# A 1 KB load ahead of the first weight load of a one-token decode kernel

## The chip, the core and the metric

The kernel runs on one core of a Trainium2 chip. The core has a matrix engine (TensorE, PE in the profile), a vector engine (VectorE, DVE), a scalar engine (ScalarE, ACT), GpSimd (POOL) and SyncE (SP), and 16 DMA engines that bring data from HBM into on-chip memory. The metric is device time in microseconds (us); less is better. "ns" is written where nanoseconds are meant.

## What is computed

One token goes through two branches that are mixed by a gate. Branch A is attention over the last 4096 positions of a key and value cache (32 query heads, 8 cache heads of 128); branch B is a gated two-layer network. Everything is in bf16.

```
def _A_ref(x, k_cache, v_cache, wq, wo):            # x 1x512
    W = min(4096, max(256, Sk // 4))                # 4096 of 65536
    q = (x @ wq).reshape(B, Sq, 32, 128) ...
    k, v = last W positions of the caches, each head repeated 4 times
    scores = einsum("bhqd,bhkd->bhqk", q, k) * (Dh ** -0.5)
    return (softmax(scores) @ v) ... @ wo           # 4096x512
def _B_ref(x, w_gate, w_up, w_down):                # 512x1792, 512x1792, 1792x512
    return (sigmoid(x @ w_gate) * (x @ w_up)) @ w_down
g = sigmoid((x * gate_w).sum(-1, keepdims=True))
return g * a + (1 - g) * b
```

With a single token there is hardly any reuse: each of the 30.67 MB of weights and cache is read from HBM once and used once.

## The kernel before

All large loads are issued by SP on one queue (`dq = nc.sync`, L78), in the order in which they are needed; each DMA engine works through its share of them in that order. The order is:

- `wq_sb` (L81): the query weights, 4 MB. `wq_v` lays them out so that partition p holds rows 4p to 4p+3 of the matrix, 32 KB in one piece.
- four `kn` (L85, called from L92): the keys, 2 MB each, two cache heads to a load.
- `wg_sb` (L95), `wu_sb` (L99) and four small `wx_sb` (L106): the two input weights of branch B.
- three `vv` (L85, from L116), then half of `wo_sb` (L118), the last `vv` in two halves (L119, L120) and the other half of `wo_sb` (L121). `vv` uses the four buffers of `kn` again (pool `blk`), so a `vv` load waits until the transposes of that `kn` are done.
- four pieces of `wd_sb` (L126), the last of them one eighth of the first.

ACT issues two loads of 1 KB on a queue of its own: x (L75) and `gate_w` (L76), both into `xr`. At the end SP and ACT each store half of the result (L367, L369).

The compute follows the loads. PE turns x into columns (L156, L163), DVE works out the gate (L173 on), and when `wq_sb` has landed PE makes q (L208). Then come the transposes of the keys on DVE (L196), the scores on PE (L235), branch B's products (L251), the softmax, the products with the values (L319), and at the end the rows of `wo_sb` and `wd_sb` (L306) summed into one result row, which DVE and ACT copy out (L366, L368).

Small tiles that live all through the kernel come from the pool `const`, one buffer each; `xr` is one of them. Tile names, pools and waits on semaphores are handled by the tile framework; only the order on PE, DVE and ACT is written out by hand (from L185 on).

Of the kernel before, what the change touches and what calls it, by code (L numbers as in the profile page):

```python
# [12 lines left out]
BF16 = mybir.dt.bfloat16  # L13
# [4 lines left out]
def kernel(  # L18
# [16 lines left out]
    P = 128  # L35
# [27 lines left out]
    const = ctx.enter_context(tc.tile_pool(name="const", bufs=1))  # L63
# [14 lines left out]
    dq = nc.sync  # L78
    wq_sb = big.tile([P, DC, HQ * DH], BF16, name="wq_sb", tag="big")
    wq_v = A_wq.rearrange("(p c) n -> p c n", c=DC)  # L80
    dq.dma_start(wq_sb[:], wq_v)  # L81


# [316 lines left out]
```

## Time and profile before

| what | value |
|---|---|
| median of 5 runs | 80.77 us (80.68 to 82.05) |
| the profiled execution's own time | 80.74 us |
| its span, first to last instruction | 79.1 us |
| granted TensorE clock, mean | 0.957 |
| busy: PE, DVE, ACT, POOL | 70%, 50%, 14%, 5% |
| bytes on SP's load queue | 30.67 MB in 2754 packets |
| HBM read over the span | 388 GB/s |

The span is smaller than the time, because the time also has what lies ahead of the first and behind the last instruction. The profile cuts the span into 40 equal slices and gives the busy share of each engine in tenths; the row DMA is the mean over the 16 DMA engines. An instruction that issues a DMA is listed under its engine with a q (SPq, ACTq): its time is the issuing alone, not the transfer. In a table of stretches the columns are: length, busy time of PE, PEld (weight loads of PE), DVE, ACT and POOL with their number of instructions, granted clock, DMA share, and GB/s; the bytes of a packet are counted in the stretch in which it starts.

### The profile page before, as it was taken

What the parts mean: (1) busy time and instruction counts of PE and PEld (TensorE: products, weight loads), DVE (VectorE), ACT (ScalarE), POOL (GpSimd) and SP (SyncE); (2) the same over time, 40 slices, a digit from 0 to 9 for tenths busy, and PEclk for the clock granted to TensorE, in tenths of its full rate; (3) what the DMA queues carried; (4) which work ended last, traced back from release to release, by engine and by line L of the source; (5) the groups of instructions that cost most, each with busy time, mean ns of one, the idle gap of its engine ahead of it and who ended that gap; (6) DMA issues with size and microseconds to landing.
All of it is one profiled execution on the core that took longest, in us unless ns stands there. A gap on an engine that the chain in (4) does not pass through costs nothing.

```text
span 79.1 us, 825 instructions
## 1 busy us (share of the span) xinstructions
PE 55.8 (70%) x324; PEld 25.6 (32%) x324; DVE 39.2 (50%) x51; ACT 11.4 (14%) x21; POOL 3.7 (5%) x13
## 2 busy tenths in 40 slices
PE   0200092999980799988899662999799569998940
PEld 0200041334420234433333230444244513475710
DVE  0600920009738999999995727999900200001020
ACT  2400000142675000000000248000200000020010
POOL 7910000000000000000000000000000000000000
PEclk9999999999999559999999999999999955999999
DMA  7599799999999999999999999999999999999700
GB/s 183 199 414 498 315 497 398 398 423 447 456 398 423 447 456 398 444 406 418 438 415 414 431 456 406 423 431 456 414 414 406 414 452 435 414 394 399 294 7 1
DMA packets 2762, 30.71 MB, mean 388 GB/s; under 512 B 324, under 2 KB 584, under 8 KB 840
## 3 DMA queue, kind: packets, MB, share of 16 engines
q1 hardware_dynamic: 2754, 30.67, 92.6%
q8 instruction: 2, 0.03, 0.2%
q10 hardware_dynamic: 6, 0.00, 0.0%
HBM read 30.67 MB, written 0.00 MB: 388 GB/s over the span
## 4 chain that ended last, share of the span: by engine, by line
DMA 91%; SPq 3%; PE 1%; DVE 1%; issue 0%
DMA kn<-in_A_k_cache_dram 38%; DMA wd_sb<-in_B_w_down_dram 30%; DMA vv<-in_A_v_cache_dram 24%; SPq L85 2%; PE a_ps L306 1%; SPq L81 1%; DVE res L366 1%
## 5 line engine op out<-in xcount | busy, mean ns | idle before, releaser
L235 PE MATMUL S_ps<-kT,qbig 128*128 128x512 bf16 x64 | 16.3, 407 | 3.9 <-DVE qbig L224 2.8
L319 PE MATMUL pv_ps<-vv,eT 128*32 128x512 bf16 x64 | 15.9, 405 | 3.3 <-DVE eT L280 1.4
L196 DVE STREAM_TRANSPOSE kT<-kn 128x2048 f32<-128x2048 f32 x8 | 17.8, 2279 | 0.0
L235 PEld LDWEIGHTS <-qbig 128*128 128x128 bf16 x64 | 6.5, 102 | 13.7 <-issue 4.5
L208 PE MATMUL q_ps<-wq_sb,xT 128*128 128x512 bf16 x32 | 9.8, 483 | 1.5 <-DMA wq_sb<-in_A_wq_dram 1.5
L319 PEld LDWEIGHTS <-eT 128*32 128x32 bf16 x64 | 6.3, 101 | 11.9 <-issue 3.8
L213 DVE STREAM_TRANSPOSE qtT<-q_sb 128x512 f32<-128x512 f32 x4 | 2.8, 700 | 8.2 <-ACT q_sb L210 8.2
L331 DVE TENSOR_TENSOR oT<-o_ps,rb 128x16 bf16<-128x16 f32 x2 | 0.3, 175 | 12.6 <-PE o_ps L330 12.6
L208 PEld LDWEIGHTS <-xT 128*128 128x128 bf16 x32 | 3.8, 120 | 7.9 <-issue 5.9
L190 PE MATMUL S_ps<-ident,other 2*128 2x512 bf16 x4 | 2.0, 610 | 6.0 <-DVE other L148 6.0
L210 ACT CAST q_sb<-q_ps 128x512 bf16<-128x512 f32 x8 | 4.7, 586 | 8.3 <-PE q_ps L208 8.3
L306 PE MATMUL a_ps<-wo_sb,oY 128*1 128x256 bf16 x64 | 4.8, 272 | 0.3 <-DVE oY L339 0.3
L325 ACT COPY pv_sb<-pv_ps 64x512 f32<-64x512 f32 x2 | 1.2, 579 | 19.4 <-PE pv_ps L319 19.4
L280 DVE STREAM_TRANSPOSE eT<-e_sb 128x1024 bf16<-128x1024 bf16 x2 | 2.4, 1224 | 1.9 <-ACT e_sb L278 1.9
L262 ACT ACTIVATE sge<-gu_ps 128x448 f32<-128x448 f32 x1 | 0.5, 544 | 18.9 <-PE gu_ps L251 18.9
L306 PEld LDWEIGHTS <-oY 128*1 128x1 bf16 x64 | 2.8, 83 | 1.2 <-DVE oY L339 0.4
L173 DVE TENSOR_TENSOR gpr<-xr 1x512 f32<-1x512 bf16 x1 | 0.7, 680 | 4.8 <-DMA xr<-in_gate_w_dram 4.8
L290 DVE RECIPROCAL sg<-sge 128x448 f32<-128x448 f32 x1 | 3.0, 2952 | 0.0
L257 DVE TENSOR_REDUCE pm<-S_ps 128x1 f32<-128x1024 f32 x2 | 2.4, 1204 | 0.9 <-PE S_ps L235 0.9
L156 PE MATMUL xt_ps<-ident,xr 1*128 1x1 bf16 x4 | 0.3, 166 | 3.5 <-POOL ident L132 3.5
L190 PEld LDWEIGHTS <-other 2*128 2x128 bf16 x4 | 0.6, 158 | 6.3 <-DVE other L148 6.1
L366 DVE CAST res<-a_ps 1x256 bf16<-1x256 f32 x1 | 0.4, 411 | 4.0 <-PE a_ps L306 4.0
(63 smaller groups left out, 34.7 us busy)
## 6 DMA issues: line engine op xcount, KB each, us to landing
kn<-in_A_k_cache_dram SPq DMA_DIRECT2D x4, 2048.0 KB, 27.8
vv<-in_A_v_cache_dram SPq DMA_DIRECT2D x3, 2048.0 KB, 18.6
wq_sb<-in_A_wq_dram SPq DMA_DIRECT2D x1, 4096.0 KB
wo_sb<-in_A_wo_dram SPq DMA_DIRECT2D x2, 2048.0 KB
vv<-in_A_v_cache_dram SPq DMA_DIRECT2D x2, 1024.0 KB
wg_sb<-in_B_w_gate_dram SPq DMA_DIRECT2D x1, 1792.0 KB, 33.5
wu_sb<-in_B_w_up_dram SPq DMA_DIRECT2D x1, 1568.0 KB
wd_sb<-in_B_w_down_dram SPq DMA_DIRECT2D x1, 1024.0 KB
```

The lines of the kernel that those rows point to most:

```text
L85: dq.dma_start(t[:, n0:n1, :].rearrange("p n d -> p (n d)"), cache[0, 2 * a:2 * a + 2, SBASE:SBASE + W, :] .rearrange("y (x n) d -> x y n ...
L190: nc.tensor.matmul(S_ps[u // 2][:, u % 2, :], lhsT=other[:].rearrange("p o y u -> p (o y u)"), rhs=ident[0:2, 0:2].rearrange("p (o y) -> p ...
L196: nc.vector.transpose(t[:].bitcast(F32), kn[a][:, v * KB:(v + 1) * KB, :] .rearrange("p n d -> p (n d)").bitcast(F32))
L208: nc.tensor.matmul(q_ps[:], lhsT=xT[:, c:c + 1].to_broadcast([P, P]), rhs=wq_sb[:, c, ks], start=(c == 0), stop=(c == DC - 1))
L210: nc.scalar.copy(q_sb[:, ks], q_ps[:])
L213: nc.vector.transpose(qtT[:].bitcast(F32)[:, kq], q_sb[:].bitcast(F32)[:, kq])
L235: nc.tensor.matmul(S_ps[v][:, hb, :], lhsT=q_st[:, a, dhi, :, t], rhs=k_v[:, hb * 16:(hb + 1) * 16, dhi, :, t], start=False, stop=(a == HP ...
L257: nc.vector.tensor_reduce(pm2[:, v:v + 1], S_ps[v][:].rearrange("p a b -> p (a b)"), axis=AX.X, op=ALU.max)
L280: nc.vector.transpose(eT[:, :, v * KB:(v + 1) * KB, :].rearrange("p a n r -> p n a r"), e_sb[:, v, :].rearrange("p (n a r) -> p n a r", a= ...
L290: nc.vector.reciprocal(sg[:], sge[:])
L306: nc.tensor.matmul(a_ps[32 * i:32 * i + 1, i, 0:HN], lhsT=lhsT, rhs=rhs[:, i * HN:(i + 1) * HN], start=start, stop=stop)
L319: nc.tensor.matmul(pv_ps[32 * (a % 2):32 * (a % 2) + 32, a // 2, :], lhsT=eT[:, a, 4 * m:4 * m + 4, :].rearrange("p n r -> p (n r)"), rhs= ...
```

## The change

A tile of 32 bf16 columns, `first`, is taken from the pool `const`. Ahead of the load of `wq_sb`, SP issues a load of 64 bytes into each of 16 of its partitions (every eighth), from the beginning of the rows of `wq_v` that belong to those partitions. Nothing reads the tile. All else stays as it is.

```
     wq_sb = big.tile([P, DC, HQ * DH], BF16, name="wq_sb", tag="big")
     wq_v = A_wq.rearrange("(p c) n -> p c n", c=DC)
+    first = const.tile([P, 32], BF16, name="first")
+    dq.dma_start(first[0:P:8, :], wq_v[0:P:8, 0, 0:32])
     dq.dma_start(wq_sb[:], wq_v)
```

More of the change, by code (lines that the diff above doesn't have):

```diff
@@ L80 @@
     wq_v = A_wq.rearrange("(p c) n -> p c n", c=DC)
+    first = const.tile([P, 32], BF16, name="first")
+    dq.dma_start(first[0:P:8, :], wq_v[0:P:8, 0, 0:32])
     dq.dma_start(wq_sb[:], wq_v)
```

## The prediction

> **What bounds the kernel now.** I read the page's slices first, then the chain of waits, then that chain in order of time, and last the opening microseconds as a timeline and as stretches of 0.25 us.
>
> ```profile
> DMA  7599799999999999999999999999999999999700
> GB/s 183 199 414 498 315 497 398 398 423 447 456 398 423 447 456 398 444 406 418 438 415 414 431 456 406 423 431 456 414 414 406 414 452 435 414 394 399 294 7 1
> ```
>
> Each digit is 1.98 us. From the third slice to the 37th the 16 DMA engines are busy without a hole. Only the first two slices move less than 200 GB/s; the rest stay around 420.
>
> ```profile
> DMA 91%; SPq 3%; PE 1%; DVE 1%; issue 0%
> DMA kn<-in_A_k_cache_dram 38%; DMA wd_sb<-in_B_w_down_dram 30%; DMA vv<-in_A_v_cache_dram 24%; SPq L85 2%; PE a_ps L306 1%; SPq L81 1%; DVE res L366 1%
> ...
> 33.11 18.62 DMA vv<-in_A_v_cache_dram
> 51.75 23.83 DMA wd_sb<-in_B_w_down_dram
> 75.58 0.04 issue
> 75.62 0.66 PE a_ps L306 x6
> 76.28 0.40 DVE res L366
> ```
>
> The chain is one queue of loads: 30.67 MB through SP's queue, the last rows of wd landing at 75.58, and only 0.66 us of matmuls, a 0.40 us copy and the output store behind it. PE (70%) and DVE (50%) have slack everywhere. So whatever moves the whole stream of loads by some time moves the end by that time, and whatever stays beside the stream costs nothing. The change stands at the head of that stream.
>
> ```profile
> 0.73 0.51 ACTq L75 DMA_DIRECT2D xr<-in_A_x_dram  x1
> 0.74 0.41 SPq L81 DMA_DIRECT2D wq_sb<-in_A_wq_dram  x1
> 1.21 2.59 SPq L85 DMA_DIRECT2D kn<-in_A_k_cache_dram  x4
> 1.28 0.21 ACTq L76 DMA_DIRECT2D xr<-in_gate_w_dram  x1
> ```
>
> ```profile
> 1.50:1.75 0.25, 0.00 (x0) 0.00 (x0) 0.00 (x0) 0.22 (x1) 0.25 (x1) 1.00 0.01 4
> 1.75:2.00 0.25, 0.00 (x0) 0.00 (x0) 0.01 (x1) 0.25 (x1) 0.25 (x1) 1.00 6.35 1573
> 2.00:2.25 0.25, 0.00 (x0) 0.11 (x1) 0.25 (x2) 0.25 (x1) 0.25 (x1) 1.00 1.01 262
> ...
> 3.75:4.00 0.25, 0.19 (x2) 0.10 (x2) 0.00 (x0) 0.00 (x0) 0.25 (x3) 1.00 2.77 1180
> 4.00:4.25 0.25, 0.00 (x0) 0.00 (x0) 0.00 (x0) 0.00 (x0) 0.25 (x2) 1.00 1.24 524
> ...
> 5.00:5.25 0.25, 0.00 (x0) 0.00 (x0) 0.00 (x0) 0.00 (x0) 0.00 (x0) 1.00 3.39 1442
> ```
>
> The last column counts a packet's bytes where it starts. 1573 GB/s for 0.25 us is 393 KB, twelve packets of 32 KB (one partition's row of wq each): twelve of the 16 engines begin their first packet at 1.75 to 2.00. Their second packets begin at 3.75 to 4.25 (1180 and 524 are nine and four packets), the third at 5.00 to 5.25. A first packet thus takes about 2.0 us and a second about 1.25: the stream loses some 0.75 us in its first packet. That is what the tiny load could touch. The line at 1.50 holds x's single kilobyte (4 GB/s): it runs at once and its readers start at 1.99.
>
> **The change, part by part.** It adds one SP instruction ahead of L81, 16 rows of 64 bytes, and a 64-byte column of the const pool. Nothing is removed, nothing reads the tile.
>
> *The issue on SP.* Everything on SP behind it moves: wq, four kn, wg, wu, the wx, vv, wo, wd and the output store. Only wq's move matters, because from kn on the issues lead the data by microseconds (wu is issued by 4.93, 14 MB stand ahead of it, some 30 us). The trace holds no issue of 16 rows. The nearest rows:
>
> ```profile
> L126 SPq DMA_DIRECT2D wd_sb<-in_B_w_down_dram x4: 328/328/430, 43.9 to 56.6; - x4
> L106 SPq DMA_DIRECT2D wx_sb<-in_B_w_up_dram x4: 676/694/822, 13.5 to 23.3; - x4
> L367 SPq DMA_DIRECT2D out_dram<-res x1: 278/278/278, 76.7 to 76.7; - x1
> ```
>
> The smallest issue on SP is 0.28 us (one row), two plain dimensions as here give 0.33 (wd), and wx, with its many-dimensioned source, 0.69. Between two issues lies 0.06 (1.15 to 1.21). The first issue of a queue seems dearer: on ACT the same form took 0.51 first and 0.21 second. If a part of wq's 0.41 is of that kind, it goes over to the tiny load and wq falls to the 0.34 of wo_sb's first half. So the delay is at least 0.28 + 0.06 - 0.07 = 0.27 and at most 0.82 + 0.06 = 0.88. I take the row that is nearest in form, wd: 0.33 + 0.06 - 0.04 (half of that saving) = 0.35 us. It lies bare on the path: no byte of the queue can flow before wq's issue.
>
> *The tiny packets.* One packet and one count of the semaphore per engine. x's load has the same 1 KB in all and ran in the line at 1.50, 0.3 to 0.5 us after its issue's end; the tiny rows will run at about 1.5 to 1.7, wq's first row at 1.8 + 0.35 = 2.15. They are over by then: 0. If they were not, a 1 KB packet is the nearest thing: the last wd rows have that size, and at the 294 GB/s of the slice near the end one on each engine, 16 KB, takes 0.06 us.
>
> *The semaphore turn.* SP already stops for earlier loads: L106's first issue waits 8.6 us, from 4.93 to 13.51, for wq. The loads seem to share a set of semaphores in turn, and one more load at the front shifts who waits for whom: wg, wu or wx may now wait for x, gate_w or the tiny load. Behind that wait stand wx, vv and the rest. x lands by 1.99 and gate_w by 8.06, when its reader starts, both before 13.51, and some 30 us of queued bytes cover the stop: 0. With that cover gone a stop for gate_w would cost up to 3 us.
>
> *Other engines.* wq lands 0.35 later (13.5 to 13.85), so the q matmuls start later, and so do the transposes that free the kn buffers for vv. vv's first issue at 28.47 still has over 10 us of queued bytes ahead: 0. gate_w may slip in ahead of wq's packets and free DVE sooner, off the path: 0.
>
> *The first packet.* What it becomes is the unknown. Bounds: it keeps its 2.0 us (0), or falls to the second's 1.25 (-0.75); slower than 2.0 is not excluded, but a packet that begins in as full a rush as now has no reason to be. I take 0, for two reasons. x's load, on a cold engine and a cold queue, showed no slow start: 0.75 us from its issue's end (1.24) to its readers (1.99). So what is slow is not the first touch but the first rush, 16 engines asking for 32 KB rows at the same moment, and the tiny load leaves that rush as it is, 0.35 us later. Second, if a first touch did cost 0.75 us, the tiny load would have to sit it out itself, on the same engine and ahead of wq, so little could be won.
>
> The Trainium skill, page "DMA: Bandwidth & Descriptors", section "Anatomy of one DMA", puts a fixed cost of about 2.0 us on each DMA of the GpSimd path, most of it the confirmation of the write, and its rules call transfers under 64 KB overhead. Were that cost in series with the queue, the sum would be 82.7; x's load took 1.26 us from issue to reader here, and 22 loads on one queue leave no hole in the slices, so it overlaps. The same page, "Latency and other measured facts", has an HBM access at 0.2 us on average and 2 us under high load; that reading of the slow first packet leaves it slow, and leaves the sum at 81.1.
>
> **Sum.** 80.74 (span 79.1 and 1.64 around it) + 0.35 + 0 + 0 + 0 = 81.09. The profiled run is 0.03 below the median of the runs, 80.77, so 81.1 stands for either.
>
> **The rivals.**
>
> *The first packet becomes a normal one* (faster). Place: the first descriptor of wq on each engine. Price: -0.75 + 0.35 = -0.40, 80.35. It decides once more than 0.35 of the 0.75 is saved. For it: every engine's second packet is quick, though the rush of 16 goes on. Against: x's quick load.
>
> *A start-up time that runs from the first touch* (same). The tiny load, issued in 0.33 where wq takes 0.41, touches HBM some 0.08 us earlier, the wait of 0.75 runs while SP issues wq, and wq's first packet ends 0.08 us sooner or as now: 80.66 to 80.8. For it: 0.35 is less than 0.75, so the whole delay could hide. Against: x again, and the twelve engines' near-equal first packets whichever of them had carried x.
>
> *A dear first issue* (slower yet). If 16 strided rows are described like wx, the delay is 0.69 + 0.06 = 0.75: 81.5. For it: ACT's first issue of 0.51. Against: two plain dimensions.
>
> *The load does nothing at all*, since its packets and issue hide in the start: excluded on SP, whose issues run back to back from 0.74.
>
> **How the numbers follow.** The main forecast has 0.52, the normal first packet 0.22, the start-up time from first touch 0.18, the dear issue 0.08. The likeliest gives 81.1, its own range 80.95 to 81.4. To leave no more than 2 in 10 out the range goes down to the full saving and up to the dear issue: 80.3 to 81.5. A measurement tells about 0.3%, 0.24 us, from no change. Slower by more: 0.52 and 0.08, less some 0.05 for a short issue: 0.55. Faster by more: 0.22 plus a little of the start-up case: 0.24. The rest, 0.21, is within.
>
> **What would show it.** SP's first line should be the tiny issue at 0.74, about 0.33 long, wq's at about 1.13. Stretches of 0.25 us should show twelve or more first packets at about 2.1 and the second ones 2.0 later, at 4.1 to 4.4; wq's readers should start near 13.9 and the last of wd land near 75.9. If second packets begin 1.25 after the first, the forecast is wrong by the saving; if wq's issue is not later than 1.0, by the delay. A stall of SP that empties the queue, seen as a hole in the DMA row after the second slice, would undo all of it.

## The result and the profile after

The changed kernel is slower. Over 44 runs its median is 82.57 us (81.37 to 82.87) against 80.86 us (80.49 to 82.06) over 79 runs of the kernel before; the ratio is 1.0112, with a 95% interval of 1.0094 to 1.0130, that is 0.9 us. Executions of every kernel here but e10 fall into two groups some 1 us apart (23 of these 44 and 20 of these 79 into the upper one), so the medians given below are those of the lower group: 81.64 against 80.81, 0.83 us more. The forecast was 81.1 us with a range of 80.3 to 81.5: the direction was right, the size was not, and the time lies outside the range by either median as by the ratio (80.8 x 1.0112 = 81.7).

The profile of the changed kernel (82.69 us, span 81.0) first as SP's issues, in the columns start, length, engine and line:

```profile
0.73 0.63 SPq L82 DMA_DIRECT2D first<-in_A_wq_dram  x1
1.42 0.57 SPq L83 DMA_DIRECT2D wq_sb<-in_A_wq_dram  x1
2.04 2.60 SPq L87 DMA_DIRECT2D kn<-in_A_k_cache_dram  x4
...
5.84 18.51 SPq L108 DMA_DIRECT2D wx_sb<-in_B_w_up_dram  x4
```

The tiny load takes 0.63 us to issue, and wq behind it 0.57 instead of 0.41. wq's issue ends at 1.99 instead of 1.15: 0.84 us later, made of 0.63, a gap of 0.06 and 0.16 for wq's own issue, less 0.01 of an earlier start. The same kernel in stretches of 0.25 us (last column: GB/s, a packet's bytes counted where it starts):

```profile
2.00:2.25 0.25, 0.00 (x0) 0.10 (x1) 0.25 (x2) 0.25 (x1) 0.25 (x1) 1.00 0.04 2
2.25:2.50 0.25, 0.00 (x0) 0.00 (x0) 0.25 (x2) 0.25 (x1) 0.25 (x1) 1.00 0.04 6
2.50:2.75 0.25, 0.00 (x0) 0.00 (x0) 0.25 (x2) 0.25 (x1) 0.25 (x1) 1.00 4.01 1049
2.75:3.00 0.25, 0.00 (x0) 0.00 (x0) 0.25 (x3) 0.03 (x1) 0.25 (x1) 1.00 2.52 655
...
4.50:4.75 0.25, 0.10 (x1) 0.10 (x2) 0.23 (x3) 0.00 (x0) 0.00 (x0) 1.00 2.16 918
4.75:5.00 0.25, 0.25 (x1) 0.25 (x1) 0.00 (x0) 0.00 (x0) 0.00 (x0) 1.00 2.48 1049
...
5.75:6.00 0.25, 0.25 (x2) 0.12 (x1) 0.21 (x2) 0.00 (x0) 0.00 (x0) 1.00 2.47 1049
6.00:6.25 0.25, 0.25 (x2) 0.00 (x0) 0.22 (x2) 0.00 (x0) 0.00 (x0) 1.00 2.15 918
```

The tiny rows run at 2.1 to 2.4 (2 and 6 GB/s), ahead of every byte of wq. The rush of wq's first packets that stood at 1.75 now stands at 2.50. Their second packets start 2.0 us later and the third 1.25 us after that, as before: the slow first packet is untouched, on DMA engines that had just carried a row of the same tensor on the same queue. In the trace's packet records the first byte of wq moves at 2.64 instead of 1.79, 0.85 us later, and a first packet takes 1.94 us (median of the 16) against 2.03. Both are within what such packets take without a load ahead of them: 1.76 to 1.92 in e2, e3, e7 and e10.

The rest of the stream is only shifted. The page's DMA row and rate for the changed kernel:

```profile
DMA  0998997999999999999999999999999999999200
GB/s 1 260 420 356 518 437 340 412 453 429 412 453 429 412 453 429 425 425 416 427 435 429 404 437 429 429 429 437 420 408 408 429 445 437 408 390 374 106 0 1
```

The first slice is empty; after it there is no hole. How this execution ends is no measure of the loss: late in it PE's clock was halved for 6.8 us (64.1 to 70.9), against 3.4 us (63.5 to 66.9) in the profile of before. The end is read instead from two experiments that differ by the change alone, e7 and e8.

### The profile page after: what moved, and what is told of

The parts are those of the page before. It is cut to its first block, busy times and chain, and to the rows that moved or that the text cites. A ratio compares the mean times of both kernels' runs of the same rounds, so it can differ in the third digit from the quotient of the medians.

```text
span 81.0 us, 826 instructions
## 1 busy us (share of the span) xinstructions
PE 57.1 (70%) x324; PEld 26.0 (32%) x324; DVE 38.8 (48%) x51; ACT 11.4 (14%) x21; POOL 3.9 (5%) x13
## 4 chain that ended last, share of the span: by engine, by line
DMA 59%; PE 16%; DVE 14%; issue 4%; SPq 3%; DVEq 0%
DMA kn<-in_A_k_cache_dram 31%; DMA vv<-in_A_v_cache_dram 28%; DVE kT L198 13%; PE pv_ps L321 8%; PE a_ps L308 7%; SPq L87 2%; PE o_ps L332 1%; SPq L82 1%; SPq L83 1%; DVE res L368 0%; DVE oY L341 0%; PE oY_ps L339 0%; DVEq L198 0%
## 5 line engine op out<-in xcount | busy, mean ns | idle before, releaser
L321 PE MATMUL pv_ps<-vv,eT 128*32 128x512 bf16 x64 | 17.4, 435 | 3.6 <-DMA vv<-in_A_v_cache_dram 1.5
L321 PEld LDWEIGHTS <-eT 128*32 128x32 bf16 x64 | 6.8, 108 | 13.4 <-issue 5.8
L215 DVE STREAM_TRANSPOSE qtT<-q_sb 128x512 f32<-128x512 f32 x4 | 2.8, 712 | 13.9 <-ACT q_sb L212 13.9
L163 DVE COPY xp<-xr 1x64 bf16<-1x64 bf16 x2 | 1.3, 1214 | 2.0 <-DMA xr<-in_A_x_dram 2.0
L294 DVE SCALAR_TENSOR_TENSOR h_sb<-gu_ps,gg,sg 128x448 bf16<-128x448 f32 x1 | 2.2, 2183 | 0.1
L280 ACT ACTIVATE e_sb<-S_ps,nb 128x1024 bf16<-128x1024 f32 x2 | 2.2, 1110 | 0.0
```

Of the source, the lines that this page charges most:

```text
L215: nc.vector.transpose(qtT[:].bitcast(F32)[:, kq], q_sb[:].bitcast(F32)[:, kq])
L280: nc.scalar.activation(e_sb[:, v, :], S_ps[v][:].rearrange("p a b -> p (a b)"), AF.Exp, bias=nb[:], scale=scale, accum_out=rs2[:, v:v + 1])
L294: nc.vector.scalar_tensor_tensor(h_sb[:].rearrange("p j i -> p i j"), gu_ps[1][:, 0:FQ].rearrange("p (i j) -> p i j", j=NJ), gg[:, 1:2], s ...
L321: nc.tensor.matmul(pv_ps[32 * (a % 2):32 * (a % 2) + 32, a // 2, :], lhsT=eT[:, a, 4 * m:4 * m + 4, :].rearrange("p n r -> p (n r)"), rhs= ...
```

## The experiments

Theory: SP's issue time ahead of wq is the whole loss, one to one. Rivals: the tiny load costs by something other than its place (packets, the semaphore turn), or the end is lost on PE. For the price of the issue itself: its form, its place as first, or sharing with ACT. All times are of the kernels as changed, in us; "issue" is the tiny load's on its queue, "bytes" the first packet of wq in the trace.

| run | issue | wq's issue | bytes | ratio to before, interval |
|---|---|---|---|---|
| before | - | 0.41 | 1.79 | 1 |
| e1 changed kernel | 0.63 | 0.57 | 2.63 | 1.0107 (1.0058 to 1.0156) |
| e2 on ACT | 0.55 | 0.40 | 1.78 | 0.9958 (0.9914 to 1.0002) |
| e3 behind wq | 0.60 | 0.41 | 1.77 | 0.9982 (0.9912 to 1.0053) |
| e4 128 rows | 0.41 | 0.41 | 2.23 | 1.0070 (1.0021 to 1.0120) |
| e5 16 adjacent | 0.39 | 0.40 | 2.23 | 1.0082 (1.0048 to 1.0116) |
| e6 one row | 0.32 | 0.37 | 2.11 | 1.0088 (1.0041 to 1.0134) |
| e7 before, x by GpSimd | - | 0.41 | 1.78 | 0.9997 (0.9948 to 1.0047) |
| e8 changed, x by GpSimd | 0.64 | 0.57 | 2.62 | 1.0092 (1.0054 to 1.0130) |
| e9 step in the source only | 0.39 | 0.40 | 2.21 | 1.0140 (1.0101 to 1.0180) |

The time follows the start of wq's bytes. Where they begin 0.32 us later (e6) the median rises by 0.30, where they begin 0.42 to 0.44 later (e4, e5, e9) by 0.4 to 0.6, and where they begin 0.84 later (e1) by 0.86. Where they begin no later (e2, e3, e7) it does not rise.

**e1, the changed kernel again.**

> The changed kernel itself once more. Theory (the load of wq is issued later, and the whole stream with it): wq's first packets begin 0.85 us later than before (2.64 against 1.79 in the profiles), they still take about 2.0 us, and an execution whose end hangs on the loads is 0.85 us longer: about 81.65 against 80.8. Rival (the end is lost on PE, whose clock is halved for 6.8 us in the profile at hand): without that stretch the time would be within 0.2 us of before.

The profiled execution took 81.43 us, 0.69 above the 80.74 of before, with PE's clock halved late for 3.4 us (65.1 to 68.6), no longer than before, and the median rose by 0.86. The rival falls: the loss is there without the long stretch. Yet this execution does end on PE and not on the last load:

```profile
43.32 21.43 DMA vv<-in_A_v_cache_dram
64.75 0.04 issue
64.79 5.20 PE pv_ps L321 x16
...
73.33 3.57 PE a_ps L308 x60
76.90 0.40 DVE res L368
```

PE starts on a piece of `vv` at 64.79 where it started at 64.04 before, 0.75 us later, and has hardly a pause from there to the copy. The delay still came with the loads, but on a path in which PE has little slack.

**e2, the same load issued by ACT behind gate_w.**

```
-    dq.dma_start(first[0:P:8, :], wq_v[0:P:8, 0, 0:32])
+    nc.scalar.dma_start(first[0:P:8, :], wq_v[0:P:8, 0, 0:32])
```

> The same 16 rows, issued by ACT behind x and gate_w instead of by SP ahead of wq. Theory (only SP's issue of wq matters): wq is issued at 0.74 again, its bytes begin at 1.8, and the time is that of before, 80.8 within 0.15. Rival (the load itself costs, by its packets, its semaphore in the turn, or the extra instruction): 81.65 still, or at least 81.1.

The loss is gone, though the 16 packets and the count of loads are the same. ACT's issues in this run:

```profile
1.27 0.21 ACTq L76 DMA_DIRECT2D xr<-in_gate_w_dram  x1
1.52 0.55 ACTq L82 DMA_DIRECT2D first<-in_A_wq_dram  x1
```

The tiny issue is dear here too, third in its queue and not first: 0.55 against 0.21 for gate_w's single row.

**e3, the load on SP's queue, but behind wq.**

```
-    dq.dma_start(first[0:P:8, :], wq_v[0:P:8, 0, 0:32])
     dq.dma_start(wq_sb[:], wq_v)
+    dq.dma_start(first[0:P:8, :], wq_v[0:P:8, 0, 0:32])
```

> The same load on SP's queue, but behind wq and ahead of the keys. Theory (only wq's issue matters; later issues have microseconds of queued bytes as cover): 80.8 within 0.15, kn issued some 0.5 us later for nothing. The tiny issue itself shows whether 0.63 us is the price of being first: 0.63 if it is the price of this form, about 0.35 if it is the price of the first place. Rival (16 packets of 64 bytes and a semaphore on every engine hold the stream up): 81.1 or more.

No loss is seen: wq's bytes begin at 1.77, and the 0.60 us more on SP ahead of the keys is covered by them. Only four runs stand behind the ratio, so its interval is 0.6 us wide to either side. And 0.60 in the second place is no price of the first place.

**e4, 64 bytes for all 128 partitions; e5, 16 adjacent partitions from 16 adjacent rows; e9, 16 adjacent partitions from every eighth row.** All ahead of wq, in place of the changed kernel's line:

```
-    dq.dma_start(first[0:P:8, :], wq_v[0:P:8, 0, 0:32])
+    dq.dma_start(first[:], wq_v[:, 0, 0:32])              e4
+    dq.dma_start(first[0:16, :], wq_v[0:16, 0, 0:32])     e5
+    dq.dma_start(first[0:16, :], wq_v[0:P:8, 0, 0:32])    e9
```

> 64 bytes for each of the 128 partitions instead of every eighth, still ahead of wq on SP: the form of the wq and wd loads, whose issues took 0.41 and 0.33 us. Theory that 0.63 us is the price of the form with steps of eight partitions: the issue falls to about 0.4, wq's bytes begin near 2.3 and the time is about 81.3. Theory that a second issue right behind a first is dear whatever its form: the two issues together still take about 1.2 us and the time is 81.65.

> The tiny load into 16 adjacent partitions from 16 adjacent rows, ahead of wq. Theory that the step of eight partitions makes the issue dear: it falls from 0.63 to about 0.41 and wq's own from 0.57 to 0.41, as with 128 rows; wq's bytes begin near 2.25 and the time is about 81.25. Theory that 16 rows instead of 128 make it dear: 0.63 and 0.57 again, 81.65.

> The rows are taken from every eighth row of wq's view again, but go into 16 adjacent partitions. Theory that the step over SBUF partitions makes the issue dear: 0.40 for the tiny load and 0.41 for wq, bytes from 2.25, time 81.25. Theory that the step in the source does: 0.63 and 0.57, 81.65.

SP's issues in e4, which moves eight times the rows, and in e9, which differs from the changed kernel only in where its rows land:

```profile
0.73 0.41 SPq L82 DMA_DIRECT2D first<-in_A_wq_dram  x1
1.20 0.41 SPq L83 DMA_DIRECT2D wq_sb<-in_A_wq_dram  x1
```

```profile
0.73 0.39 SPq L82 DMA_DIRECT2D first<-in_A_wq_dram  x1
1.19 0.40 SPq L83 DMA_DIRECT2D wq_sb<-in_A_wq_dram  x1
```

So it is neither the number of rows nor the step in the source. Nor is it the number of DMA engines: in the changed kernel, e4, e5 and e9 alike the trace has 16 landings for the tiny load, one for each engine. The step of eight over the partitions of the destination makes the issue 0.63 instead of 0.39, and the issue behind it 0.57 instead of 0.40. With adjacent partitions wq's bytes begin 0.42 to 0.44 later than before. e5's profiled execution took 81.14 and e9's 81.33, against 81.43 in e1; e9's ratio takes in all of its runs, 81.24 to 82.46; its median rises by 0.53.

**e6, one row on one DMA engine.**

```
+    dq.dma_start(first[0:1, :], wq_v[0:1, 0, 0:32])
```

> One row of 64 bytes on one DMA engine, ahead of wq. Theory (the price is the time SP needs to issue ahead of wq): with an issue like that of the output store, 0.28, and wq at 0.41, wq begins 0.34 later and the time is 81.1 to 81.2. If an issue on fewer than 16 engines is dear, as the four wx of 0.69 may be, 0.6 or more and 81.5 or more.

Even the cheapest load tried ahead of wq costs 0.32 us of issue and a gap, with 0.04 won back on wq's own issue (0.37): bytes begin 0.32 later, and the median rises by 0.30, near the 0.34 of the theory. A price for few engines is not seen.

**e7 and e8, x and gate_w issued by GpSimd, in the kernel before and in the changed one.**

```
-    nc.scalar.dma_start(xr[:, 0, :], A_x[0, :, :])
+    nc.gpsimd.dma_start(xr[:, 0, :], A_x[0, :, :])        (gate_w the same)
```

> The kernel before, with x and gate_w issued by GpSimd, so that ACT issues nothing while SP issues wq. Rival for the price of an issue (SP and ACT share the unit that makes descriptors, and ACT's 0.51 at the same moment lengthens SP's): wq's issue falls from 0.41 to about 0.33 and the time by up to 0.1. Theory (the price is that of the form): 0.41 and 80.8 as before.

> The changed kernel with x and gate_w issued by GpSimd. Rival (sharing with ACT): the tiny issue falls from 0.63 to 0.4 or less, and the time to 81.4. Theory (form): 0.63 and 0.57 as in the changed kernel, 81.65.

With ACT out of the way SP's issues stay as they were: 0.41 in e7, 0.64 and 0.57 in e8. Sharing with ACT falls. The pair also shows how the loss travels. The chains of waits in order of time, e7 first, then e8:

```profile
51.80 23.77 DMA wd_sb<-in_B_w_down_dram
75.58 0.04 issue
75.62 0.65 PE a_ps L306 x6
76.26 0.40 DVE res L366
```

```profile
52.74 23.71 DMA wd_sb<-in_B_w_down_dram
76.45 0.04 issue
76.50 0.64 PE a_ps L308 x6
77.13 0.40 DVE res L368
```

wq's first bytes are 0.84 us apart (1.78 and 2.62), the landings of the wd piece that the chain waits for 0.87 (75.58 and 76.45), and the matmuls and the copy behind them take the same. Some 75 us of queued loads hand the delay through whole. The profiled times are 1.09 apart (80.66 and 81.75); the other 0.2 us lies behind the copy.

**e10, the kernel before with the wx loads laid over 16 DMA engines.** A trial of the one-to-one rule in the other direction: time taken off the fullest engines.

```
-    wx_v = B_w_up.rearrange("(h b j i c) f -> h b i j c f", h=2, b=2, j=4, i=8)[:, :, :, :, DC - 1, FH:F]
+    wx_v = B_w_up.rearrange("(h b p c) f -> h b p c f", h=2, b=2, p=32)[:, :, :, DC - 1, FH:F]
...
-        nc.vector.tensor_copy(xp[:, h, :].rearrange("o (b i j) -> o b i j", b=2, j=4),
-                              xr[:, 0, :].rearrange("o (h b j i c) -> o h b i j c", h=2, b=2, j=4, i=8)[:, h, :, :, :, DC - 1])
+        nc.vector.tensor_copy(xp[:, h, :],
+                              xr[:, 0, :].rearrange("o (h p c) -> o h p c", h=2, p=64)[:, h, :, DC - 1])
```

> The kernel before with the four wx loads laid out over all 16 DMA engines (rows in plain order) instead of, as the trace's counts of packets suggest, 8; x's copy for them is put in the same order. Theory (the end hangs on the fullest DMA engine's queue, so a time moved there moves the end one to one, in either direction): 16 rows of 1792 bytes at 0.075 us, 1.2 us, lie on 8 engines now, 0.6 us on 16, and the time falls by 0.6 to about 80.2. Rival (the end hangs on the sum that all engines share, or on PE): 80.8 as before.

A miss: the time did not fall to 80.2. All six runs lie between 82.03 and 82.46, and the ratio is 1.0152 (1.0088 to 1.0216). Around the wx rows, e10 first, then the kernel before:

```profile
40.50:41.00 0.50, 0.20 (x2) 0.10 (x1) 0.50 (x2) 0.00 (x0) 0.00 (x0) 1.00 1.77 407
41.00:41.50 0.50, 0.50 (x3) 0.19 (x2) 0.50 (x1) 0.00 (x0) 0.00 (x0) 1.00 0.20 44
41.50:42.00 0.50, 0.50 (x4) 0.24 (x3) 0.42 (x1) 0.00 (x0) 0.00 (x0) 1.00 1.36 466
42.00:42.50 0.50, 0.50 (x4) 0.15 (x2) 0.00 (x0) 0.00 (x0) 0.00 (x0) 1.00 0.64 262
```

```profile
40.50:41.00 0.50, 0.50 (x4) 0.21 (x3) 0.50 (x1) 0.00 (x0) 0.00 (x0) 1.00 1.20 478
41.00:41.50 0.50, 0.36 (x2) 0.08 (x1) 0.50 (x1) 0.00 (x0) 0.00 (x0) 1.00 1.24 487
41.50:42.00 0.50, 0.35 (x2) 0.19 (x2) 0.50 (x2) 0.00 (x0) 0.00 (x0) 1.00 1.15 492
42.00:42.50 0.50, 0.50 (x4) 0.20 (x2) 0.50 (x1) 0.00 (x0) 0.00 (x0) 1.00 1.06 426
```

Before, half of the engines go on with 16 KB packets of vv while the other half carry wx rows. In e10 all 16 carry wx rows, and hardly a packet starts in the half microsecond from 41.0: the packet records have the 16 first packets of vv at 1.0 to 1.2 us instead of 0.61, and 54 of the 128 wx rows at 0.10 to 0.20 instead of 0.074. What the spreading was to save, some 0.6 us, is about what each engine loses in its first vv packet (0.4 to 0.6 us), and the wd piece that the chain waits for lands at 76.91.

That the spreading made the kernel slower is not shown. With the wx loads as they were, one engine can fall behind at the same place: in e2's profile (81.81 us, wq's bytes at 1.78) one packet of wu took 1.02 us instead of 0.47, one engine landed its share of wu at 41.90 where the other 15 had landed theirs by 40.52, and the wd piece landed at 76.60. The longer runs of the kernel before, beside e10's, took 81.74 to 81.88 us, 0.3 less than e10's median of 82.13, and the ratio sets e10 against the shorter ones. Why packets are slow there stays open.

**e11, wq as two loads, the first of 8 KB per partition.**

```
-    dq.dma_start(wq_sb[:], wq_v)
+    dq.dma_start(wq_sb[:, 0:1, :], wq_v[:, 0:1, :])
+    dq.dma_start(wq_sb[:, 1:DC, :], wq_v[:, 1:DC, :])
```

> The kernel before with wq's load as two loads, the first quarter of each partition's row (8 KB) and the other three (24 KB). If the slow first packet is a fixed start-up of 0.75 us, the first packets of 8 KB take 0.31 + 0.75, about 1.05 us, and the stream is as late as before: 80.8. If it is a rate at which 16 engines begin (32 KB in 2.0 us), they take about 0.5 us, the slow phase goes on in the packets behind them, and the time is 80.8 as well; if the slow phase ends with the first packet, whatever its size, 0.5 us are saved: 80.3.

The first 16 packets took 0.31 to 1.08 us, 0.71 in the median, and nearly all the others 0.31 to 0.35. A first packet of 8 KB thus lost some 0.4 us; one of 32 KB loses 0.5 to 0.8 (medians of 1.76 to 2.03 against 1.24 for the second packets, in the five kernels that have no load ahead of wq). That is less than a fixed 0.75, and the slow phase is mostly over with the first packet, but with this spread one profile does not show that the loss depends on the size. The ratio is 0.9994 (0.9942 to 1.0045), so a gain at the end is not shown.

## Why the prediction was right or wrong

**The bound: right.** One queue of loads sets the end, and a shift at its head arrives whole (e7 and e8: 0.84 in, 0.87 out). Two readings of it were too generous. PE does not have "slack everywhere": in e1 the end hangs on PE's last 12 us of work. And 75.58 is the landing of the third of the four wd pieces; the fourth, issued at 56.64, lands 19.3 us later, at 75.9.

**The issue on SP: the step that failed.** The prediction bounded it by 0.27 and 0.88, took the wd row "nearest in form" and got 0.35. It measured 0.84 to 0.85 (0.63 for the tiny issue, a gap of 0.06, and 0.16 more for wq's own). The form was misjudged: two plain dimensions, but the destination steps over partitions, and that alone makes 0.63 of 0.39 (e9). With adjacent partitions it would have been 0.42 to 0.44 later, near the 0.35 and inside its own range of 80.95 to 81.4 (e5: 81.14). A second piece went the wrong way: wq's issue was to fall by 0.04 in second place; it did so behind one row (0.37, e6), stayed at 0.40 to 0.41 behind the plain loads (e4, e5, e9) and rose to 0.57 behind the stepped one. The thought of a dear first issue, taken from ACT's 0.51 and 0.21, is not borne out on SP: wq takes 0.41 first (before) and 0.41 second (e4).

**The range.** Its upper end, 81.5, was the "dear issue" rival at 0.75, with a chance of 0.08. The step's own upper bound, 0.88, makes 80.74 + 0.88 = 81.62, which the range left out, and which is what came (81.64). The row that bore on it was there: wx at 0.69 showed that an issue can cost twice another one.

**The tiny packets: right, 0.** They end at 2.36 us in the profile of the changed kernel, before wq's first at 2.64; behind wq (e3) or on ACT's queue (e2) they cost nothing either.

**The semaphore turn: right, 0.** It did shift: the first wx issue came at 5.84 instead of 13.51, earlier, not later.

**Other engines: right.** gate_w slipped in ahead of wq (its packet at 2.43 instead of 6.43) and DVE began on it at 2.79 instead of 8.06, for nothing at the end. The sign that wq's readers would start near 13.9 came true (13.9) by luck: their start hangs on the engine that lands wq last, which came late in the profile of before (readers from 13.5, against 13.0 in e2 and 13.2 in e3, whose wq is issued as early).

**The first packet: right, 0.** Its medians are 1.81 to 2.00 us in the seven profiles with the load ahead of wq, and 1.76 to 2.03 in the five without one (before, e2, e3, e7, e10). That kills the rivals of a normal first packet (80.35; the sum gives 80.34) and of a start-up time from first touch (80.66 to 80.8): rows that begin 0.4 to 0.5 us ahead, one or eight for each engine (in e6 one row on one engine), changed nothing. The reason given, a first rush of 16 engines, is not shown. In e10 packets slow down in mid-run, where nothing is cold, when the engines come from wx to vv; but when all 16 engines turn from wq to the keys, at 12.6 to 12.9 us in the same run, no packet is slow.

What stays open: why the step over partitions slows its own issue and the next one, and what makes the first packets slow, or those of vv in e10. No kernel here was shown to be faster than the one before.

## What to carry to other kernels

In a kernel that one queue of loads bounds from start to end, whatever is issued on that queue ahead of the first large load costs its issue time in full, however few bytes it moves; the same load behind the first large one (e3), or on another engine's queue (e2), cost nothing here. Price an issue by the way its on-chip side is laid out, not by its rows or bytes, and where two rows of issue times differ by a factor of two, carry both to the ends of the range. A warm-up must be shown something to warm: here the small load of x at the start, quick from the first, already hinted that there was nothing.

## What was not expected of the hardware

- An issue of 16 rows into every eighth partition takes 0.55 to 0.64 us on SP and ACT, one of 128 rows into adjacent partitions 0.41, and 16 into adjacent ones 0.39; behind the stepped one wq's issue takes 0.57 instead of 0.40 (e1, e4, e5, e8, e9).
- The wx loads issue in 0.33 us with the rows in plain order (e10) and in 0.69 with the nested order of before.
- Spreading small rows over all 16 DMA engines saved nothing: the 16 first packets of the next load took 1.0 to 1.2 us instead of 0.61 (e10; 44 GB/s worth of packets started in half a microsecond, against 487).
- With the rows as they were, one packet of wu took 0.93 to 1.02 us instead of 0.47 in e2, e6 and e9. In e2 and e6 one engine landed wu over 1.2 us behind the other 15.
